# Chunk 0 of a delta-rule layer: the diagonal score blocks by products of their own, turned by VectorE, and loads in another order

## The chip, the cores and the metric

The kernel runs on one core of one Trainium2 chip. The metric is the device time of one execution in microseconds (us). Before the change it is 650.69 us, the median of three runs (650.61, 650.69 and 657.98).

## The reference

A linear attention with the delta rule (4 batches, 8 heads, 768 tokens, 48 elements a head) feeds a feed-forward block (3072 tokens, 384 wide, 2048 hidden):

```python
k_n = k / (np.linalg.norm(k, axis=-1, keepdims=True) + 1e-06)
state = np.zeros((B, H, D, D), dtype=np.float32)
for t in range(S):
    kt, vt, bt = (k_n[:, :, t], v[:, :, t], beta[:, :, t, None])
    y[:, :, t] = np.einsum('bhd,bhde->bhe', q[:, :, t], state)
    v_old = np.einsum('bhde,bhd->bhe', state, kt)
    state = state + bt[:, :, :, None] * np.einsum('bhd,bhe->bhde', kt, vt - v_old)
...
h = x @ w_in            # x: y with the heads side by side
g = h * (1.0 / (1.0 + np.exp(-h)))
return (g @ w_out).astype(np.float32)
```

## The kernel before

The tokens are cut into six chunks of 128. Within a chunk the recurrence is solved in closed form: each half of 64 tokens needs the inverse of a triangular 64x64 matrix made of the keys' products, beta and the keys' lengths. The inverse is built from 32x32 diagonal blocks: for each of the 32 pairs of batch and head and each of the four 32-token blocks, one 32x32 block stands on one partition of VectorE's layout (128 partitions of 1024 elements), and VectorE eliminates column after column there. Small matmuls of 32x32 tiles (`corner`, `turned`, `straight`, `merge_half`) then join the blocks. All matmuls are float32; one matmul of the program shows in the trace as two loads of weights and two matmuls.

What chunk 0 needs before its first state update is the start of the kernel:

- `load_k(0)` and `load_q(0)` bring keys and queries on SyncE's queue; beta comes on ScalarE's queue. `turn` (L481) transposes the keys of one batch b on TensorE, and VectorE or ScalarE copies them out of PSUM.
- `first_score` multiplies the keys of each 64-token half with themselves (`score`, L504) and copies the products into the tiles `ap`. `block_out` (L557) writes the 32x32 diagonal blocks of `ap` to DRAM in eight DMAs, and `block_in` reads them back, one block a partition, as `g`.
- `square` (L361) squares the keys on GpSimd, `add_squares` (L375) sums them on VectorE, and `norm_steps` (L383) makes from the sums the lengths `n` and the steps -beta/n^2 with some sixteen small VectorE instructions. `block_steps` (L430) brings the steps into the layout of the blocks with one TensorE product.
- `invert_first` (L651) multiplies the corners of `g` by the steps (L656), eliminates 15 columns (L664, L668), and transposes the result on VectorE (L678, L682). Between its steps TensorE turns the keys of chunk 1, and `busy` issues matmuls whose result nobody reads.
- `first_queries` turns the queries, multiplies keys by queries, and masks the result, on VectorE for the first half of the batches.
- `joins(0, ...)` runs the small matmuls of one half, with a list of things to do between its stages (parts of the narrowing of `w_in`, the scaling of v by `size_half`). Then follow `inner`, `first_outputs`, `update`, and the first hidden products (`phid`, L1029).

The order on each engine is the program's: `pin` ties each instruction to the one before it on its engine. DMAs of SyncE are in line as well; `linked` makes the next one wait until the last one before it has landed. The weights come as 768 KB pieces: `fetch_w_in(i)` loads, and `narrow` converts on ScalarE, VectorE and GpSimd.

PSUM has eight banks in three rotating groups, A (three), CC (three) and M (two); `bank(room, name)` takes the next of a group. The banks of CC are kept tiles, one each.

The order of loads behind the queries is

```python
    fetch_w_in(0)
    load_k(1)
    fetch_w_in(1)
    load_v(0)
    ...
    linked(fetch_w_in, 2)
    linked(load_q, 1)
    fetch_w_in(3)
    linked(fetch_w_in, 4)
```

and it stands behind `block_in(0)` in SyncE's queue.

Of the kernel before, what the change touches and what calls it, by code (L numbers as in the profile page):

```python
# [19 lines left out]
def kernel(  # L20
# [10 lines left out]
    nc = tc.nc  # L31
# [26 lines left out]
    A, CC, M = deque(("a0", "a1", "a2")), deque(("c0", "c1", "c2")), deque(("m0", "m1"))  # L58
    kept_banks = {tag: banks.tile([P, 512], FP32, name=f"pb_{tag}", tag=tag) for tag in CC}

    def bank(room, name):

        tag = room[0]
        room.rotate(-1)
        return kept_banks.get(tag) or banks.tile([P, 512], FP32, name=name, tag=tag)

# [101 lines left out]

    def linked(fetch, *args):

        pace.append(line[-1])
        fetch(*args)
# [173 lines left out]

    def beta_of(c):
        pb = bank(A, "pb")
        pin(nc.tensor.transpose(
            pb[:, 0:BH], beta_fm[:, c].rearrange("n s t -> n (s t)"), ident[0:BH, 0:BH]  # L350
        ))
        pin(nc.scalar.activation(
            out=beta_tok[:, c, :].rearrange("p (n e) -> p e n", e=2),
            in_=pb[:, 0:BH].rearrange("p (e n) -> p e n", e=2), func=ACTF.Copy,
        ))
# [26 lines left out]

    def norm_steps(c):  # L383

        seed, t, r = (small.tile([P, BH], kind, name=name, bufs=1)[:] for name, kind in (
            ("seed", U32), ("nt", FP32), ("nr", FP32)
        ))
        ss = sums.pop(c)
        n = small.tile([P, BH], FP32, name="n", bufs=1)
        by_slot = small.tile([P, 2, B * NP], FP32, name="n_slot", bufs=1)  # L390
        yield pin(nc.vector.tensor_scalar(
            out=seed, in0=ss.bitcast(U32), scalar1=-0.5, scalar2=1597463007.0,
# [12 lines left out]
        yield pin(nc.vector.tensor_tensor(out=t, in0=r, in1=ss, op=ALU.mult))  # L405
        yield pin(nc.vector.tensor_scalar(out=n[:], in0=t, scalar1=1e-6, scalar2=None, op0=ALU.add))
        yield pin(nc.vector.reciprocal(out=r, in_=n[:]))
        yield pin(nc.vector.tensor_tensor(out=t, in0=r, in1=beta_tok[:, c, :], op=ALU.mult))
# [133 lines left out]
    def block_room(c):  # L542

        if c == 0:
            g, x = (sum_room[:, at : at + T * T] for at in (AT_G, AT_X))
        else:
            g = work.tile([P, T * T], FP32, name="g", tag="g", bufs=1)[:]
            x = (
                sum_room[:, AT_LAST : AT_LAST + T * T] if c == 1
                else work.tile([P, T * T], FP32, name="x", tag="x", bufs=1)[:]  # L550
            )
        pin(nc.gpsimd.memset(x, 0.0))
        pin(nc.gpsimd.memset(x[:, 0 : T * T : T + 1], 1.0))
        g, x = (t.rearrange("p (s t) -> p s t", t=T) for t in (g, x))
        blocks[c] = (tc.dram_tile([P, T, T], FP32, name=f"blocks{c}"), g, x)

# [87 lines left out]

    Q, ys = T // 2, {}

# [4 lines left out]
    def invert_first(step):  # L651
# [33 lines left out]
        both = work.tile([P, BH, T], FP32, name="xe_y", tag="g", bufs=1)  # L685
        xes[0], ys[0] = both[:], both[:].rearrange("p (g h) t -> p g h t", g=2)

        def heads(g, hf):
            for i in range(HH // 2):
                for e in range(2):  # L690
                    yield i, HH * g + 2 * i + e, hf ^ e ^ g

        def of_half(t, g, hf, k):
            return t[:, HH * g + (hf ^ k ^ g) : HH * (g + 1) : 2]

# [3 lines left out]
        def corner(g, hf):  # L699

            pls = [bank(room, "pl") for room in (A, CC)]
            for i, n, k in heads(g, hf):
                for j in (2 * k, 2 * k + 1):
                    cols = slice(T * (j % 2), T * (j % 2 + 1))
                    pin(nc.tensor.matmul(
                        pls[k][rows[j], Q * i : Q * (i + 1)], lhsT=aps[0, g][0][rows[j], n % HH // H, n % H, cols],
                        rhs=low[rows[j], n, :], start=True, stop=True,
                    ))
                    yield
# [7 lines left out]
        def turned(g, hf):  # L717

            pls = [bank(room, "pl") for room in (A, CC)]
            for i, n, k in heads(g, hf):  # L720
                pin(nc.tensor.matmul(
                    pls[k][rows[2 * k], T * i : T * (i + 1)], lhsT=up[rows[2 * k], n, :],
                    rhs=y[rows[2 * k], n, :], start=True, stop=True,
                ))
                yield
# [3 lines left out]
        def straight(g, hf):  # L729

            pls = [bank(room, "pl") for room in (A, CC)]
            for i, n, k in heads(g, hf):
                for j in (2 * k + 1, 2 * k):
                    pin(nc.tensor.matmul(
                        pls[k][rows[j], T * i : T * (i + 1)], lhsT=y[rows[j], n, :],
                        rhs=up[rows[j], n, :], start=True, stop=True,
                    ))
                    yield
            for odd in (1, 0):
                for k, by in enumerate((by_act, by_dve)):  # L740
                    j = 2 * k + odd
                    by(
                        of_half(xi[rows[j]].rearrange("p g h t -> p (g h) t"), g, hf, k)[:, :, T * odd : T * odd + T],
                        out_of(pls[k], rows[j], T),
# [36 lines left out]
    def merge_half(g, hf, second):  # L781

        y = ys[0][:, g]
        pms = [bank(room, "px" if second else "py") for room in (A, CC)]
        for i in range(HH // 2):
            for e in range(2):
                n, k = 2 * i + e, hf ^ e ^ g
                even, odd = slice(W * k, W * k + T), slice(W * k + T, W * (k + 1))
                if second:
                    to, left, right = even, y[odd, n, :], xis[g][odd, n, T:W]  # L790
                else:
                    left = aps[0, g][0][even, n // H, n % H, T:W]
                    to, right = odd, xes[0][even, g * HH + n, :]
                yield pin(nc.tensor.matmul(
                    pms[k][to, T * i : T * (i + 1)], lhsT=left, rhs=right, start=True, stop=True
                ))
        for k, by in enumerate((by_act, by_dve)):
            e, half = hf ^ k ^ g, slice(W * k, W * k + T) if second else slice(W * k + T, W * (k + 1))
            of = pms[k][half, 0 : HH // 2 * T].rearrange("p (h t) -> p h t", t=T)
            by(xis[g][half, e::2, T:W] if second else y[half, e::2, :], of)  # L800

# [250 lines left out]
    def project():  # L1052

        rooms = [A.popleft(), CC.popleft()]
        pos = [bank(M, "po") for n in range(HB)]
        pos += [kept_banks.get(tag) or banks.tile([P, 512], FP32, name="po", tag=tag) for tag in rooms]
        o = mlp.tile([P, HB, DM], FP32, name="o", bufs=1)
# [204 lines left out]

    def first_score(b):

        def evacuate(j, e, to, of):
            (by_dve if e else by_act)(to, of)

        score(0, b, (0,), (A, CC), evacuate)
        if b % HB == 1:
            block_out(0, b // HB)  # L1270

    busy(3)
    for b in range(B):
        square(0, b)
    block_room(0)
    for b in range(2):
        turn(0, b, 0, M, b % 2 == 0)
    first_score(0)
    for b in range(2, B):
        turn(0, b, 0, M, b % 2 == 0)  # L1280
    for b in range(1, B):
        first_score(b)
        add_squares(0, b - 1)
    add_squares(0, B - 1)
    beta_of(0)

    def first_queries(b):

        def evacuate(j, e, to, of):
            (mask if b < HB else by_act)(to, of)  # L1290

        turn(0, b, 1, M)
        score(0, b, (1,), (A, CC), evacuate)

    block_in(0)
    busy(4)
    for _ in norm_steps(0):
        pass
    for b in range(2):
        first_queries(b)  # L1300
        busy(1)
    for t in xis:
        pin(nc.gpsimd.memset(t, 0.0))
    step = block_steps(0)
    fetch_w_in(0)
    load_k(1)
    fetch_w_in(1)
    load_v(0)
    for c in range(1, NCH):
        beta_of(c)  # L1310
    busy(1)
    for b in range(2, B):
        first_queries(b)
# [127 lines left out]
    sums_made = sum_w()  # L1441
    later = {}

    def script(text):
# [114 lines left out]
```

## Time and profile before

| what | value |
|---|---|
| runs | 650.61, 650.69, 657.98 us |
| profiled execution | 652.37 us, span 650.4 us |
| TensorE (PE) busy | 627.6 us, 96% of the span |
| VectorE (DVE) busy | 397.6 us, 61% |
| ScalarE (ACT) busy | 213.8 us, 33% |
| GpSimd (POOL) busy | 90.9 us, 14% |
| granted TensorE clock, mean | 0.99 |
| chain that ended last | PE 91%, DMA 2%, issue 2%, DVE 2% |
| inversion of chunk 0 (L656 to L682) | 20.71 to 34.03 us |
| first hidden product (L1029) | 52.3 us |

The times in the profile's rows are microseconds from the start of the span. A row of the chain gives start, duration and what it was; a row of the timeline gives start, busy time, engine, line, operation, output and inputs, and in brackets the idle time before it with what ended it. A row of the windows gives, after the stretch and its length, the busy time and number of instructions of PE, PE's weight loads, DVE, ACT and POOL, then the granted clock of TensorE, the DMA share, and GB/s. "Issue" is time in which the engine waited for nothing that the profile shows. PE's share is high, but the kernel's start is made of short dependent steps.

### The profile page before, as it was taken

What the parts mean: (1) busy time and instruction counts of PE and PEld (TensorE: products, weight loads), DVE (VectorE), ACT (ScalarE), POOL (GpSimd) and SP (SyncE); (2) the same over time, 40 slices, a digit from 0 to 9 for tenths busy, and PEclk for the clock granted to TensorE, in tenths of its full rate; (3) what the DMA queues carried; (4) which work ended last, traced back from release to release, by engine and by line L of the source; (5) the groups of instructions that cost most, each with busy time, mean ns of one, the idle gap of its engine ahead of it and who ended that gap; (6) DMA issues with size and microseconds to landing.
All of it is one profiled execution on the core that took longest, in us unless ns stands there. A gap on an engine that the chain in (4) does not pass through costs nothing.

```text
span 650.4 us, 21395 instructions
## 1 busy us (share of the span) xinstructions
PE 627.6 (96%) x9416; PEld 548.0 (84%) x9416; DVE 397.6 (61%) x911; ACT 213.8 (33%) x497; POOL 90.9 (14%) x92
## 2 busy tenths in 40 slices
PE   7878899999989999999999999999999999999997
PEld 5577778756779989989989989989989989889997
DVE  5875689997764987453986453987454974103112
ACT  2455663332342122451122452122451122451111
POOL 5023631334101020010020010020011000000000
PEclk9979999999989999999999999999999999999999
DMA  9876534250288324268324268324173024100101
GB/s 136 209 165 206 192 75 104 98 97 3 53 154 148 58 73 60 50 136 143 59 76 57 48 131 146 61 74 60 28 153 72 10 65 60 40 13 1 25 0 25
DMA packets 145676, 54.70 MB, mean 84 GB/s; under 512 B 117152, under 2 KB 138912, under 8 KB 145584
## 3 DMA queue, kind: packets, MB, share of 16 engines
q1 hardware_dynamic: 143136, 52.93, 39.6%
q8 instruction: 74, 1.21, 0.8%
q10 hardware_dynamic: 2448, 0.41, 0.4%
q14 instruction: 18, 0.15, 0.1%
HBM read 40.14 MB, written 11.01 MB: 79 GB/s over the span
## 4 chain that ended last, share of the span: by engine, by line
PE 91%; DMA 2%; issue 2%; DVE 2%; ACT 1%; SPq 1%; DVEq 0%
PE phid L1029 38%; PE px L1136 16%; PE py L1136 12%; PE po L1064 5%; PE pb_c L828 3%; PE pa L517 2%; PE pb_c L816 2%; PE pyc L907 2%; PE pb_c L1064 2%; PE pb_c L848 1%; PE pb_c L336 1%; PE pyc L894 1%; DMA kb<-in_k_dram 1%; PE pt L488 1%; PE py L770 1%
## 5 line engine op out<-in xcount | busy, mean ns | idle before, releaser
L1029 PE MATMUL phid<-xT,w_in 128*128 128x256 f32 x1152 | 260.1, 383 | 2.1 <-DMA xT<-part 2.0
L1029 PEld LDWEIGHTS phid<-xT,w_in 128*128 128x128 f32 x1152 | 216.9, 191 | 34.4 <-issue 3.0
L1039 ACT ACTIVATE gT<-phid 128x512 f32<-128x512 f32 x88 | 52.5, 597 | 149.8 <-PE phid L1029 145.2
L615 DVE SCALAR_TENSOR_TENSOR rank<-g,step,x 128x31 f32<-128x31 f32 (+15 forms) x124 | 49.8, 401 | 35.8 <-DMA g<-blocks 32.3
L1118 DVE TENSOR_TENSOR sums_of_g<-gT 128x384 f32<-128x384 f32 (+1 forms) x60 | 29.9, 518 | 59.0 <-ACT gT L1039 48.4
L1136 PE MATMUL py<-w_out,sums_of_g 128*128 128x192 f32 x320 | 56.8, 329 | 0.0
L1136 PE MATMUL px<-sums_of_w,sums_of_g 128*128 128x192 f32 x320 | 56.8, 329 | 0.0
L1136 PEld LDWEIGHTS px<-sums_of_w,sums_of_g 128*128 128x128 f32 x320 | 52.2, 190 | 0.5
L1136 PEld LDWEIGHTS py<-w_out,sums_of_g 128*128 128x128 f32 x320 | 52.2, 190 | 0.4
L620 DVE TENSOR_TENSOR x<-x,rank 128x31 f32<-128x31 f32 (+15 forms) x124 | 42.5, 343 | 4.3
L455 POOL TENSOR_TENSOR vf<-vf,n_slot 128x768 f32<-128x768 f32 x10 | 15.0, 1516 | 169.3 <-DMA vf<-in_v_dram 125.3
L476 DVE STREAM_TRANSPOSE kq<-stage 128x512 f32<-128x512 f32 x28 | 28.5, 1114 | 12.0 <-DMA stage<-in_q_dram 10.4
L532 ACT COPY xT<-pyc 48x128 f32<-48x128 f32 (+2 forms) x126 | 32.6, 259 | 1.6
L1136 PE MATMUL px<-sums_of_w,gT 128*128 128x192 f32 x160 | 28.4, 329 | 0.0
L1136 PE MATMUL py<-w_out,gT 128*128 128x192 f32 x160 | 28.4, 329 | 0.0
L1136 PE MATMUL px<-w_out,gT 128*128 128x192 f32 x160 | 28.0, 327 | 0.0
L1136 PEld LDWEIGHTS px<-w_out,gT 128*128 128x128 f32 x160 | 26.4, 190 | 0.5
L538 POOL COPY g<-x 64x256 f32<-64x256 f32 x4 | 5.0, 1241 | 154.5 <-DVE x L623 154.5
L1136 PEld LDWEIGHTS py<-w_out,gT 128*128 128x128 f32 x160 | 26.1, 190 | 0.3
L1136 PEld LDWEIGHTS px<-sums_of_w,gT 128*128 128x128 f32 x160 | 26.1, 190 | 0.2
L828 PEld LDWEIGHTS pb_c<-vf,xi 64*64 64x64 f32 x736 | 23.5, 138 | 3.2 <-issue 2.9
L1147 DVE TENSOR_TENSOR o<-o,kept 128x192 f32<-128x192 f32 (+1 forms) x29 | 11.5, 422 | 24.0 <-ACT kept L1144 24.0
(221 smaller groups left out, 921.6 us busy)
## 6 DMA issues: line engine op xcount, KB each, us to landing
vf<-in_v_dram SPq DMA_DIRECT2D x48, 96.0 KB, 3.2
out_dram<-o SPq DMA_DIRECT2D x42, 96.0 KB, 2.2
w_out<-in_moe_w_in_dram SPq DMA_DIRECT2D x4, 768.0 KB, 4.4
sums_of_w<-in_moe_w_out_dram SPq DMA_DIRECT2D x4, 768.0 KB, 5.9
blocks<-ap SPq DMA_DIRECT2D x44, 64.0 KB, 1.9
g<-blocks SPq DMA_DIRECT2D x5, 512.0 KB, 3.5
kb<-in_k_dram SPq DMA_DIRECT2D x12, 192.0 KB, 5.1
kb<-in_k_dram SPq DMA_DIRECT2D x24, 96.0 KB, 4.6
```

The costliest lines, as they stand in the source:

```text
L455: pin(nc.gpsimd.tensor_tensor(out=vf, in0=vf, in1=of, op=ALU.mult))
L476: pin(nc.vector.transpose(out=kqs[c, b][:, :, j, :].rearrange("p a (i m) -> p a m i", i=T), in_=src.rearrange("p a (m d) -> p a m d", d=D) ...
L517: pin(nc.tensor.matmul(pa[e][half, p * n * W : (p + 1) * n * W], lhsT=kq[rows, p, 0, half], rhs=kq[rows, p, js[0] : js[-1] + 1, half], sta ...
L532: return pin(nc.scalar.copy(to, of))
L615: pin(nc.vector.scalar_tensor_tensor(out=tv, in0=g[:, 0:m, m : m + 1].to_broadcast([P, m, n]), scalar=step[:, m : m + 1], in1=x[:, m : m + ...
L620: yield pin(nc.vector.tensor_tensor(out=x[:, 0:m, m:T], in0=x[:, 0:m, m:T], in1=tv, op=ALU.add))
L828: yield pin(nc.tensor.matmul(pz[rows, n * D : (n + 1) * D], lhsT=xis[g][rows, u * H + 2 * p + e, :], rhs=vfs[c][rows, hf, g * HB + u, p, : ...
L1029: pin(nc.tensor.matmul(ph[:, j * GT : (j + 1) * GT], lhsT=w_in[:, a, (2 * f + j) * P : (2 * f + j + 1) * P], rhs=xTs[c, hf][:, a, :], star ...
L1039: pin(nc.scalar.activation(out=hidden_of(c, hf, f), in_=ph[:], func=ACTF.Silu, scale=-0.5 if in_blocks(c) else 0.5))
L1064: pin(nc.tensor.matmul(pos[i][:, 0:DM], lhsT=hidden_of(0, hf, f // 2)[:, at : at + C], rhs=w_outs[f // HFF][:, f % HFF, :], start=(f == 0) ...
L1118: pin(nc.vector.tensor_tensor(out=sums_of_g[:, k, fs], in0=of[0], in1=of[1], op=op))
L1136: pin(nc.tensor.matmul(to, lhsT=at, rhs=quarter(f, *b) if isinstance(b, tuple) else sums_of_w[b][:, f], start=start and f == 0, stop=f == ...
```

## The change

In chunk 0 the round trip through DRAM is gone. `own_products(b)` multiplies, for each head and each 32-token block, the block's keys with themselves, 32 products a batch, into one PSUM tile `double` that spans two banks (the former c0 and c1 of CC, which later stages use as its two halves). One VectorE transpose of 128x1024 elements then brings all the 32x32 blocks into the layout of `g`. The blocks' diagonals are the squared lengths: one strided copy takes them, so that the squares on GpSimd and their sums on VectorE are left out in chunk 0. Beta is transposed by TensorE and once more by VectorE into the same layout, and the step comes from two more VectorE instructions, with no TensorE product. The lengths are brought back to tokens by one VectorE transpose behind the first step of the inversion, and ScalarE copies them into slots.

The key scores of whole halves are still made, behind the own products, in the banks of A and M, and ScalarE alone copies them out. The masks of chunk 0's first half move into `joins(0, ...)`. The order of the batch-and-head index in the joins follows the new layout. `busy` always uses bank c2. The loads of `w_in` 0 and of chunk 1's keys stand right behind the queries, and the others have new links: `linked` gets an argument `back`, which names how far back in SyncE's line the awaited DMA stands.

```diff
+    double = banks.tile([P, 1024], FP32, name="pb_c01", tag="c01")
+    kept_banks = {
+        "c0": double[:, 0:512], "c1": double[:, 512:1024], "c2": banks.tile([P, 512], FP32, name="pb_c2", tag="c2")[:],
+    }
...
-    def linked(fetch, *args):
-        pace.append(line[-1])
+    def linked(fetch, *args, back=1):
+        pace.append(line[-back])
         fetch(*args)
...
-            pw = bank(CC, "pw")
+            pw = kept_banks["c2"]
...
+    def own_products(b):
+        kq = kqs[0, b]
+        for p in range(NP):
+            for j in range(NB):
+                for e in range(2):
+                    n, of, at = HH * e + NP * b + p, slice(W * e, W * e + D), slice(T * j, T * (j + 1))
+                    pin(nc.tensor.matmul(
+                        double[at, T * n : T * (n + 1)], lhsT=kq[of, p, 0, at], rhs=kq[of, p, 0, at],
+                        start=True, stop=True,
+                    ))
+
+    def first_steps(pb):
+        by_head = small.tile([P, 2, T], FP32, name="by_head", bufs=1)
+        n, beta_n = (by_head[:, i] for i in range(2))
+        pin(nc.vector.transpose(out=beta_n, in_=pb[:, 0:BH]))
+        g = sum_room[:, AT_G : AT_G + T * T]
+        pin(nc.vector.transpose(
+            out=g.rearrange("p (t s) -> p t s", s=T), in_=double[:].rearrange("p (n t) -> p t n", t=T)
+        ))
...
+        pin(nc.vector.tensor_copy(out=ss, in_=g[:, 0 : T * T : T + 1]))
+        for _ in length_steps(ss, seed, t, r, n):
+            pass
+        pin(nc.vector.tensor_tensor(out=t, in0=r, in1=beta_n, op=ALU.mult))
+        step = small.tile([P, T], FP32, name="step")
+        pin(nc.vector.scalar_tensor_tensor(
+            out=step[:], in0=r, scalar=-1.0, in1=t, op0=ALU.mult, op1=ALU.mult
+        ))
+        return step, n
+
+    def first_sizes(n):
...
+        pin(nc.vector.transpose(out=by_token[:], in_=n))
...
     busy(3)
-    for b in range(B):
-        square(0, b)
     block_room(0)
     for b in range(2):
         turn(0, b, 0, M, b % 2 == 0)
-    first_score(0)
+    pb = turn_beta(0)
+    for b in range(2):
+        own_products(b)
     for b in range(2, B):
         turn(0, b, 0, M, b % 2 == 0)
-    for b in range(1, B):
-        first_score(b)
-        add_squares(0, b - 1)
-    add_squares(0, B - 1)
-    beta_of(0)
...
-    block_in(0)
-    busy(4)
-    for _ in norm_steps(0):
-        pass
...
-    step = block_steps(0)
+    for b in range(2, B):
+        own_products(b)
+    step, norms = first_steps(pb)
     fetch_w_in(0)
     load_k(1)
-    fetch_w_in(1)
-    load_v(0)
+    linked(load_v, 0, back=1 + 2 * 3)
+    for b in range(B):
+        score(0, b, (0,), (A, M), evacuated)
+    busy(2)
+    for t in xis:
+        pin(nc.gpsimd.memset(t, 0.0))
+    linked(fetch_w_in, 1, back=8 + 1)
...
-    linked(fetch_w_in, 2)
-    linked(load_q, 1)
-    fetch_w_in(3)
-    linked(fetch_w_in, 4)
-    linked(fetch_w_in, 5)
-    linked(fetch_w_in, 6)
+    linked(fetch_w_in, 2, back=2)
+    linked(fetch_w_in, 3, back=2)
+    linked(fetch_w_in, 4, back=2)
+    linked(load_q, 1, back=2)
+    linked(fetch_w_in, 5, back=2 * 3 + 1)
+    linked(fetch_w_in, 6, back=2)
     begin(("in", 0))
     inv = invert_first(step)
     for n in range(1 + Q):
         done = next(inv)
+        if n == 0:
+            first_sizes(norms)
...
-    together(joins(0, [sized, none, none, filled(2), filled(1), none, none, filled(2), begin_next, none]))
+    together(joins(0, [sized, none, none, filled(2), filled(1), masked, none, filled(2), begin_next, none]))
```

More of the change, by code (lines that the diff above doesn't have):

```diff
@@ new lines, in first_sizes @@
+    def first_sizes(n):
+        by_token = small.tile([P, BH], FP32, name="n", bufs=1)
+        by_slot = small.tile([P, 2, B * NP], FP32, name="n_slot", bufs=1)
+        pin(nc.vector.transpose(out=by_token[:], in_=n))
+        of = by_token[:].rearrange("p (e n) -> p e n", e=2)
+        for g, rows in enumerate(HALVES):
+            ns, rest = slice(HB * NP * g, HB * NP * (g + 1)), HALVES[1 - g]
+            by_act(by_slot[rows, :, ns], of[rows, :, ns])
+            for hf in range(2):
+                by_act(by_slot[rest, hf, ns], of[rest, 1 - hf, ns])
+        sizes[0] = by_slot
@@ L405, in norm_steps @@
         yield pin(nc.vector.tensor_tensor(out=t, in0=r, in1=ss, op=ALU.mult))
-        yield pin(nc.vector.tensor_scalar(out=n[:], in0=t, scalar1=1e-6, scalar2=None, op0=ALU.add))
-        yield pin(nc.vector.reciprocal(out=r, in_=n[:]))
+        yield pin(nc.vector.tensor_scalar(out=n, in0=t, scalar1=1e-6, scalar2=None, op0=ALU.add))
+        yield pin(nc.vector.reciprocal(out=r, in_=n))
+    def norm_steps(c):
+        seed, t, r = (small.tile([P, BH], kind, name=name, bufs=1)[:] for name, kind in (
+            ("seed", U32), ("nt", FP32), ("nr", FP32)
+        ))
+        ss = sums.pop(c)
+        n = small.tile([P, BH], FP32, name="n", bufs=1)
+        by_slot = small.tile([P, 2, B * NP], FP32, name="n_slot", bufs=1)
+        yield from length_steps(ss, seed, t, r, n[:])
         yield pin(nc.vector.tensor_tensor(out=t, in0=r, in1=beta_tok[:, c, :], op=ALU.mult))
@@ L641, in invert @@
         read_up(c, up)
-    Q, ys = T // 2, {}
+    Q, ys, later = T // 2, {}, {}
     def corners(at):
@@ L719, in turned @@
             pls = [bank(room, "pl") for room in (A, CC)]
-            for i, n, k in heads(g, hf):
+            for i, _, m, k in heads(g, hf):
                 pin(nc.tensor.matmul(
-                    pls[k][rows[2 * k], T * i : T * (i + 1)], lhsT=up[rows[2 * k], n, :],
-                    rhs=y[rows[2 * k], n, :], start=True, stop=True,
+                    pls[k][rows[2 * k], T * i : T * (i + 1)], lhsT=up[rows[2 * k], m, :],
+                    rhs=y[rows[2 * k], m, :], start=True, stop=True,
                 ))
@@ L1358, in none, with masked @@
         pass
-    together(joins(0, [sized, none, none, filled(2), filled(1), none, none, filled(2), begin_next, none]))
+    def masked():
+        for u in range(HB):
+            masks(0, u)
+    together(joins(0, [sized, none, none, filled(2), filled(1), masked, none, filled(2), begin_next, none]))
     masks(1, 0)
@@ L1441 @@
     sums_made = sum_w()
-    later = {}
     def script(text):
```

83 lines of the change are left out of this document (40 added, 43 removed).

## The prediction

> **What bounds it now.** The page comes first: PE is busy for 627.6 of 650.4 us and holds 91% of the chain that ended last. The change touches only the preparation of chunk 0, so what counts is when PE gets its first dense work, and how that start is limited. I read the chain of waits from 0 to 48 us, then VectorE's timeline, the 1-us windows, and the trace's packets of the queue that carries PE's program. The chain first:
>
> ```profile
> 5.17 3.35 DMA kb<-in_k_dram
> 9.84 0.20 PE pa L517
> 12.56 0.93 DVE ss L377 x2
> 13.52 0.19 DVE seed L391
> 16.21 0.36 DVE nr L407
> 17.49 0.19 DVE spread L411
> 20.07 0.14 PE pg L433 x2
> 34.20 0.29 issue
> 36.88 1.38 issue
> 40.52 1.86 issue
> ```
>
> Keys land, PE turns and multiplies them, VectorE adds squares, makes the step sizes, PE turns those, and the inversion can begin. The two long "issue" rows are PE waiting for nothing that the profile shows. VectorE's timeline has the inversion's start (L656), its last transpose, and the work that follows:
>
> ```profile
> 20.71 0.69 DVE L656 TENSOR_TENSOR sums_of_w<-sums_of_w,step 128x512 f32<-128x512 f32 x1 [0.95 <-ACT beta_tok L352]
> 31.19 1.06 DVE L678 STREAM_TRANSPOSE sums_of_w<-sums_of_w 128x512 f32<-128x512 f32 x1
> 32.10 1.93 DVE L682 STREAM_TRANSPOSE sums_of_w<-sums_of_w 128x1024 f32<-128x1024 f32 x1
> 44.81 1.29 DVE L1326 TENSOR_TENSOR ap<-ap,above 128x512 f32<-128x512 f32 x2
> ```
>
> The windows show PE empty in both issue rows, and the clock (seventh entry) halved behind the first; the trace has it at 0.5 from 39.64 to 49.88 us, three stretches of 3.41:
>
> ```profile
> 37.00:38.00 1.00, 0.00 (x0) 0.00 (x0) 0.56 (x1) 0.00 (x0) 0.01 (x1) 1.00 0.66 117
> 38.00:39.00 1.00, 0.73 (x67) 0.74 (x68) 0.33 (x1) 0.39 (x2) 0.00 (x0) 1.00 0.88 326
> 40.00:41.00 1.00, 0.52 (x20) 0.42 (x16) 0.97 (x3) 0.41 (x2) 0.32 (x1) 0.50 0.00 0
> 41.00:42.00 1.00, 0.00 (x0) 0.00 (x0) 0.76 (x2) 0.00 (x0) 1.00 (x1) 0.50 0.38 79
> ```
>
> **PE waits for its own program.** Page part 3 has a queue q8, kind instruction, of 74 packets; in the trace each has 16,384 bytes. I numbered PE's instructions (loads, matmuls, semaphore waits) in order of time. The issue stalls stand before numbers 1217, 1473, 2241, 2497, 2753 and 4033, all 193 plus a multiple of 256, and each ends 1.2 to 1.5 us after a q8 packet (40.94 to 42.37 for instance). Passing 193+256k asks for the block that is needed 256 later. From passing to use it took 3.73 us (34.53 to 38.26), 4.11 (38.26 to 42.37), 4.25, 4.55, and 6.86 when 2.3 MB of weights were in flight (60.50 to 67.36). So 256 small instructions cannot pass faster than about 4 us.
>
> [...]
>
> **The change, start of the inversion.** Removed: squares on POOL (4 x 0.82), VectorE's four reductions (L377, 0.54 each), eight block DMAs and the one back, the spread copies, the step product pg on PE and its ACT copy, and before the inversion 16 PE instructions net of own products (3 busy matmuls of 4, one pg of 4). POOL and SP work was in the way only through the waits above. Added: 128 own products, each two loads and two matmuls by the form of L517, so 512 PE instructions, 128 per b.
> - b 0 and 1: the first products can start where L517 starts now, 7.66. Beta's last packet ended at 6.23, so its transpose before them is not late. A score's 64 instructions take 7.66 to 8.14, 7.5 ns each; L705's 112 of 32-wide tiles take 51.58 to 52.07, 4.4 ns. With 0.8 us per b (bounds 0.56 and 0.96), two end at 9.3.
> - Turns of b 2 and 3 (keys landed at 8.53): first product 1.03 later, as 8.74 to 9.77 now. So 10.3, and b 2 ends at 11.1.
> - b 3 begins at number 436, and 449 stands 13 into it. Number 193, in b 1, passes at about 8.7; now it passes at 10.35, its packet ends at 13.40, and with 1.4 more the block is there 4.45 later. The same turnaround gives 13.15, plus 0.7 for the rest: 13.85. By 3.73 it is 13.1, by 6.86 it is 16.3; with no stall 11.9.
> - VectorE turns both banks, 128x1024. Rows of that size from SBUF take 1.93 to 1.97; from PSUM none is shown. Bounds: two copies of 128x512 out of PSUM (L500, 0.69 each), 1.4, and two transposes L476 of 1.114, 2.2. I take 1.95, the same operation: 15.8.
> - The diagonal copy 0.2, the unchanged length steps L391 to L407 3.15 (13.52 to 16.67), the product with beta and the step 0.43 as L408 and one L411: the inversion starts at **19.6**, not 20.71: 1.1 earlier (range 18 to 22).
> - One 128x32 transpose now stands inside the inversion, 0.2 by the small rows of L408. Its by-product, ACT's six size copies, is hidden: ACT is idle for 1.5 us at 28.7 and POOL needs the sizes only at 35.5; uncovered they cost 6 x 0.2.
>
> [...]
>
> **Joins.** Added and removed instructions net to +496 PE instructions, 16 short of two blocks, so every later boundary falls 16 instructions further on. Now the corners (L705) begin at number 716, 11 past a boundary that was passed early; after, the boundary comes 5 into them. The next block is then asked for at the corners rather than some 1.5 us ahead, and the sequence 34.5, 38.3, 42.4 becomes about 35.5, 39.5, 43.6 on the same scale: **1.2 lost** (0 to 2.4). The two masks of chunk 0's first half (1.29 us as the L1326 row) move from before the inversion into the joins; VectorE is idle there for 1.1 and 1.0 while PE waits for its block, so I cost them at 0; without those stalls they cost up to 1.3.
>
> **Loads.** Now w_in 2 to 6 and q 1 are chained from 36 to 59 us. After, SP's queue loses five block DMAs, so w_in 0 and k 1 follow q 0 at 9.8; v waits for w_in 0 (about 17), w_in 1 stands behind v's eight issues (0.65 each), and w_in 2 to 6 follow by landings: all in flight by about 43. Keys of chunk 1 stop holding PE (its wait ends at 29.35 now). No engine waits for weights between 30 and 110 us now, so earlier weights alone gain nothing; but fetches that queue behind them do. Stalls of 0.7, 1.4 and 1.9 us at 55.2, 59.1 and 65.5 meet DMA shares near 1. With quieter engines there, I take **1.7** of these 4.0 back (0 to 3.8). The price is busier DMA in the joins, inside the 1.2's upper bound.
>
> Sum: -1.1 + 0.2 + 1.2 - 1.7 = **-1.4 us**. The profiled execution took 652.37 (span 650.4, the rest around it), so it would take 651.0; the median shown, 650.69, lies 1.7 below that execution, and becomes **649.3**.
>
> **Rivals.**
> - The block is there in time for b 3, and later stalls go too (0.2). For: b 3 follows turns and copies, which give time. Against: 449 is reached at 11.2 and no block came within 3.7. Start at 17.7, 2.8 gained with the transpose inside, joins even, 1.7 to 3.5 later: 646.2 to 644.4.
> - Slower (0.2): fetches in the joins. Weights and q 1 are in flight at 31 to 43; if a turnaround there exceeds about 4.9 us, three boundaries cost three times the excess. At 6, 3 x 1.9 = 5.7 replaces the 1.2: 653.8. For: the 6.86 came with such traffic. Against: 4.11 came at shares of 0.9.
> - The start comes earlier but the time doesn't (0.1): the fetch pace and not VectorE sets 34 to 67 us, and the quieter DMA gives nothing: 650.7.
> - The half clock lasts one stretch longer or shorter (part of the range): 3.41 at half rate is at most 1.7 either way.
>
> The forecast itself has 0.5. Two per cent, 13 us, is about what a measurement of this kernel can tell from no change; every case lies within it, so 0.95 falls there, 0.02 faster and 0.03 slower for what I have not seen, such as a wait on the two banks made into one tile. The range is 645 to 653: most of the first rival, and of the slower one the part with a turnaround up to about 5.7.
>
> **What would show it.** Right: 512 PE instructions at 7.7 to 14 us with an issue gap of 1 to 2 us before the last b; one 128x1024 VectorE transpose of about 1.95 at 14; L656's successor at 19 to 20; issue rows in the joins no shorter than now; fewer after 55. Wrong: an inversion start before 18.5 or after 21, a transpose far from 1.95, joins over 12 us after the corners, or ACT late with key copies so that the corners wait for scores.

## The result, and the profile after

The change makes the kernel slower: 688.25 us, the median of four runs (683.37 to 689.83), against 653.42 for the kernel before in runs made beside them. The ratio is 1.0513, with a 95% interval from 1.0422 to 1.0605. The forecast was 649.3 us within 645 to 653. The profiled execution of the changed kernel took 689.83 us, with a span of 688.1. Ratios here and below are of undisturbed runs only, so they are not always the quotient of the two medians.

The chain of waits of the changed kernel, in the stretch that the prediction showed of before (start, duration, what):

```profile
10.90 0.79 PE pb_c L399 x47
11.69 2.35 issue
14.04 0.79 PE pb_c L399 x44
14.83 2.28 PE pa L577 x69
17.11 2.58 issue
19.69 1.97 PE pa L577 x59
21.65 2.86 PE pb_c L339 x4
...
36.08 3.42 PE pb_c L339 x10
...
43.19 0.13 PE pl L771 x2
...
45.36 1.75 issue
```

The own products (L399) meet the block boundary of the program as forecast (2.35 us). But the chain then stays with TensorE (PE), and ScalarE's copies of the queries between its products, for 28 us. The key scores (L577) stand behind the own products and meet the next boundary (2.58). Then come two warming products that take 2.86 us, the queries one batch after the other, and the warming products of chunk 1, until the first corner (L771) at 43.12 (its piece of the chain begins at 43.19). VectorE's timeline of the same kernel shows who waits meanwhile:

```profile
14.87 1.25 DVE L410 STREAM_TRANSPOSE sums_of_w<-pb_c 128x1024 f32<-128x1024 f32 x1 [3.90 <-PE pb_c L399]
19.91 0.69 DVE L717 TENSOR_TENSOR sums_of_w<-sums_of_w,step 128x512 f32<-128x512 f32 x1
31.32 1.89 DVE L743 STREAM_TRANSPOSE sums_of_w<-sums_of_w 128x1024 f32<-128x1024 f32 x1
43.87 0.34 DVE L778 SCALAR_TENSOR_TENSOR sums_of_w<-pl,second,pick 64x128 f32<-64x128 f32 x1 [10.66 <-PE pb_c L771]
52.92 2.57 DVE L1374 TENSOR_TENSOR ap<-ap,above 128x512 f32<-128x512 f32 x2
```

The inversion starts at 19.91 (before: 20.71) and ends at 33.21 (before: 34.03). So the round trip through DRAM is indeed replaced by something quicker. Then VectorE is idle for 10.66 us, because the corners are not there; in before it went on at once. The waits over the whole span (engine, tile and line, what it waited for; us in total, times, longest), first the four longest of PE on VectorE in after, then the longest of these in the kernel b_double, which matters below:

```profile
PE pb_c L577 <- DVE ap L587: 6.9, 4, 2.8
PE pb_c L860 <- DVE xi L595: 4.7, 3, 2.5
PE pb_c L800 <- DVE xe_y L595: 1.6, 2, 1.1
PE pb_c L771 <- DVE sums_of_w L778: 0.8, 1, 0.8
```

```profile
PE pb_c L520 <- DVE ap L530: 3.7, 4, 1.4
```

`pb_c` is a bank of the group CC, of which c0 and c1 are now halves of one tile. The products wait until VectorE has copied something out of it, at places far from chunk 0 too: 2.8 us of the first row stand at about 215 us, 2.1 at about 512. The page's row of the granted clock, first of after, then of a_apart (below), shows what follows from such gaps:

```profile
PEclk9796689999999999999999999999999999989999
```

```profile
PEclk8796999999999999999999999999999999999999
```

In the trace the clock of after is at 0.5 for 58.0 us in all, in seven stretches that are multiples of 3.41 us (the first from 14.14 to 24.38, the next from 48.28 to 65.34); before has 13.7 us. The products of `phid` (L1095) start every 0.43 us from 215.6 to 218.8, at 0.50, and every 0.22 us from 224 to 226, at 1.00. So by an estimate from the granted clock the 44 us more cost at most half of that, 22 us of the 37.7 by which the spans differ.

Where the time goes, by the start of each stage (us in the span of the profiled execution; the kernels are explained below):

| kernel | inversion | first corner | first `inner` | first `phid` | span | ratio to before (95%) |
|---|---|---|---|---|---|---|
| before | 20.71 | 33.37 | 44.24 | 52.34 | 650.4 | 1 |
| after | 19.91 | 43.12 | 59.06 | 67.34 | 688.1 | 1.0513 (1.0422 to 1.0605) |
| b_double | 21.38 | 35.11 | 49.92 | 57.91 | 672.4 | 1.0287 (1.0246 to 1.0329) |
| a_apart | 19.05 | 42.02 | 55.76 | 63.56 | 659.6 | 1.0139 (1.0098 to 1.018) |
| a_pipe | 19.91 | 36.99 | 52.57 | 60.45 | 680.2 | 1.037 (1.0319 to 1.0421) |
| a_loads | 20.02 | 43.34 | 56.46 | 64.44 | 679.6 | 1.0466 (1.0409 to 1.0522) |
| both | 19.67 | 36.35 | 50.86 | 58.34 | 652.7 | 1.0006 (0.9972 to 1.004) |
| both_pad | 18.95 | 37.33 | 51.42 | 59.80 | 655.1 | 1.0045 (1.0006 to 1.0084) |
| both_warm | 18.87 | 34.28 | 48.58 | 56.29 | 653.4 | 0.9995 (0.9966 to 1.0025) |
| both_masks | 19.44 | 34.46 | 46.68 | 56.20 | 654.5 | 1.0041 (1.0002 to 1.008) |
| both_quiet | 20.02 | 35.44 | 45.65 | 61.95 | 657.9 | 1.0146 (1.0089 to 1.0203) |
| both_loads | 19.76 | 37.12 | 50.69 | 58.45 | 655.8 | 1.0049 (1.0022 to 1.0077) |
| both_q1 | 19.65 | 34.79 | 46.00 | 55.39 | 649.7 | 0.9987 (0.9947 to 1.0027) |
| both_q1_nopad | 19.00 | 33.64 | 45.11 | 54.18 | 653.7 | 1.0048 (1.0013 to 1.0084) |

The first `phid` of after comes 15.0 us late, yet the end comes 37.7 us late. So 22.7 us are lost behind the stage that the change touches.

### The profile page after: what moved, and what is told of

It reads as the page before. It is cut to its first block, busy times and chain, and to the rows that moved or that the text cites. A ratio compares the mean times of both kernels' runs of the same rounds, so it can differ in the third digit from the quotient of the medians.

```text
span 688.1 us, 21853 instructions
## 1 busy us (share of the span) xinstructions
PE 647.3 (94%) x9664; PEld 563.3 (82%) x9664; DVE 393.8 (57%) x896; ACT 216.9 (32%) x509; POOL 87.6 (13%) x88
## 3 DMA queue, kind: packets, MB, share of 16 engines
q8 instruction: 76, 1.25, 0.8%
## 4 chain that ended last, share of the span: by engine, by line
PE 87%; DVE 5%; issue 3%; ACT 2%; SPq 1%; DMA 1%; POOL 1%; DVEq 0%; POOLq 0%; ACTq 0%
PE phid L1095 37%; PE px L1202 15%; PE py L1202 11%; PE po L1130 3%; PE pb_c L894 3%; PE pa L577 2%; PE pb_c L339 2%; PE pb_c L882 2%; PE pb_c L914 1%; PE pb_c L577 1%; PE pt L548 1%; PE pyc L973 1%; SPq L161 1%; PE pyc L960 1%; DMA stage<-in_q_dram 1%
## 5 line engine op out<-in xcount | busy, mean ns | idle before, releaser
L1095 PE MATMUL phid<-xT,w_in 128*128 128x256 f32 x1152 | 267.7, 392 | 1.8 <-DMA xT<-part 1.7
L1095 PEld LDWEIGHTS phid<-xT,w_in 128*128 128x128 f32 x1152 | 223.0, 196 | 35.3 <-issue 4.3
L1105 ACT ACTIVATE gT<-phid 128x512 f32<-128x512 f32 x88 | 52.5, 597 | 159.1 <-PE phid L1095 152.5
L515 POOL TENSOR_TENSOR vf<-vf,n_slot 128x768 f32<-128x768 f32 x10 | 14.8, 1484 | 172.5 <-DMA vf<-in_v_dram 125.4
L894 PEld LDWEIGHTS pb_c<-vf,xi 64*64 64x64 f32 x736 | 25.1, 145 | 6.8 <-issue 3.3
L894 PE MATMUL pb_c<-vf,xi 64*64 64x48 f32 x736 | 27.3, 230 | 2.9 <-ACT z L592 2.3
L577 PE MATMUL pa<-kq 48*64 48x128 f32 (+1 forms) x448 | 24.3, 279 | 5.3 <-ACT kq L558 2.7
L577 PEld LDWEIGHTS pa<-kq 48*64 48x64 f32 x448 | 20.6, 158 | 8.0 <-issue 4.1
```

Source lines behind the costliest of these rows:

```text
L515: pin(nc.gpsimd.tensor_tensor(out=vf, in0=vf, in1=of, op=ALU.mult))
L577: pin(nc.tensor.matmul(pa[e][half, p * n * W : (p + 1) * n * W], lhsT=kq[rows, p, 0, half], rhs=kq[rows, p, js[0] : js[-1] + 1, half], sta ...
L894: yield pin(nc.tensor.matmul(pz[rows, n * D : (n + 1) * D], lhsT=xis[g][rows, u * H + 2 * p + e, :], rhs=vfs[c][rows, hf, g * HB + u, p, : ...
L1095: pin(nc.tensor.matmul(ph[:, j * GT : (j + 1) * GT], lhsT=w_in[:, a, (2 * f + j) * P : (2 * f + j + 1) * P], rhs=xTs[c, hf][:, a, :], star ...
L1105: pin(nc.scalar.activation(out=hidden_of(c, hf, f), in_=ph[:], func=ACTF.Silu, scale=-0.5 if in_blocks(c) else 0.5))
```

## Experiments, first round: which part of the change costs

Three theories stood against each other: T1, the two halves of one tile make products wait for copies that have nothing to do with them; T2, TensorE's queue ahead of the corners has become longer than the inversion; T3, the arrival of the program's blocks and the half clock.

**a_apart**: after, with c0 and c1 as tiles of their own from the moment that VectorE has turned the double tile. The instructions stay; the two warming products behind the key scores write to c0 and c1.

```diff
-    double = banks.tile([P, 1024], FP32, name="pb_c01", tag="c01")
+    first = ExitStack()
+    double = first.enter_context(tc.tile_pool(name="first", bufs=1, space=PSUM)).tile([P, 1024], FP32, ...)
...
     step, norms = first_steps(pb)
+    first.close()
+    pair = ctx.enter_context(tc.tile_pool(name="pair", bufs=1, space=PSUM))
+    for tag in ("c0", "c1"):
+        kept_banks[tag] = pair.tile([P, 512], FP32, name=f"pb_{tag}", tag=tag)
...
-    busy(2)
+    busy(2, tags=("c0", "c1"))
```

> The changed kernel, but the two banks of the own products are one tile only until VectorE has turned them; from then on c0 and c1 are two tiles again, and the two busy matmuls behind the key scores go to c0 and c1. Theory T1 (the shared tile: a wait on either half is a wait on both, in the joins and in every later chunk's scores): the joins, 16.0 us from the first corner to the last merge in the changed kernel, fall to 12 or less, the waits of TensorE on VectorE's masked scores (3.1 us in the window around 215 us, 2.4 around 512) are gone, and the time falls by 15 us or more, to 664 to 673. Theory T2 (TensorE's queue ahead of the corners alone) and T3 (program fetch and clock): within 4 us of 688; the first corner stays at 43 us under all three.

Measured: 662.9 us, ratio 1.0139. The first corner stays at 42.02, as T1 has it, and about 25 us are gone, a little more than T1's bound. No score waits for VectorE in this kernel, and from 60.6 us on the clock stays at 1.0 to the end, with 23.9 us of half clock in all. The joins, from first corner to first `inner`, fall from 15.9 to 13.7 us, not to the 12 that T1 expected. The pages show what the 28.5 us between the two spans are made of: the same 9664 matmuls keep TensorE busy for 647.3 us in after and for 630.9 in a_apart, 16.4 us less, and the time in which it is not busy falls by 12.1 us.

**b_double**: before, with nothing but the two banks made into halves of one tile.

```diff
+    double = banks.tile([P, 1024], FP32, name="pb_c01", tag="c01")
-    kept_banks = {tag: banks.tile([P, 512], FP32, name=f"pb_{tag}", tag=tag) for tag in CC}
+    kept_banks = {"c0": double[:, 0:512], "c1": double[:, 512:1024], "c2": banks.tile([P, 512], ...)[:]}
```

> The kernel before with one edit: banks c0 and c1 are the two halves of one tile, as in the change; nothing else. T1: slower by 8 us or more, in the joins (10.9 us now from the first corner to the last merge) and at the scores of later chunks. T2 and T3: the time of the kernel before within 2 us, since neither TensorE's queue nor its number of instructions is touched.

Measured: 673.89 us beside 654.95 for before, ratio 1.0287: 19 us for a change that adds no instruction. Four waits of scores on VectorE appear here too (3.7 us, the row above), and the joins take 14.8 us instead of 10.9. T1 holds from both sides: put in alone it costs 19 us, taken out of after it gives 25 back.

**a_pipe**: after, with the queries' serial chain (turn, ScalarE's copy, score, then the next batch) overlapped by two batches, and the four warming products between them left out.

```diff
     for b in range(2):
         turn(0, b, 1, M)
-        score(0, b, (1,), (A, CC), evacuated)
-        busy(1)
     for c in range(1, NCH):
         beta_of(c)
-    for b in range(2, B):
-        turn(0, b, 1, M)
+    for b in range(B):
         score(0, b, (1,), (A, CC), evacuated)
-        busy(1)
+        if b + 2 < B:
+            turn(0, b + 2, 1, M)
```

> The changed kernel with chunk 0's queries in another order: two batches are turned ahead, each further turn stands behind a score, and the four busy matmuls between them are left out (their result is read by nobody). T2 (turn, copy, score and busy of four batches run one after the other for 11.6 us, from 24.5 to 36.1, and push the corners to 43.1 while VectorE waits for 10.7): the four batches take 6 to 7 us, the first corner comes at 37 to 39, and the time falls by 4 to 7 us. T3 (fetch): the fetch pace holds the corners, which move by less than 2 us. T1 says nothing of the corners.

Measured: 679.51 us, ratio 1.037; the first corner at 36.99 instead of 43.12. The gain against after is 8.7 us, a little over what T2 gave.

**a_loads**: after, with the loads in before's order and with its links.

> The changed kernel with the loads in the order and with the links of the kernel before (they still stand ahead of the key scores, with no round trip of blocks before them). If the new order of loads delays the program's blocks (packets 2.4 and 1.8 us behind the passing at 14.0 and 19.7 us), the two stalls of 2.5 and 2.6 us shorten and the time falls by 2 to 5 us; if the order helps, as the prediction had it, the time grows by 1 to 4 us; T1 and T2 alone leave it within 2 us.

Measured: 685.57 us, ratio 1.0466. The interval overlaps that of after, so this run alone settles nothing; both_loads takes it up again. The two stalls ahead of the inversion did not shorten: from one TensorE instruction's start to the next they are 2.6 and 3.2 us, in after 2.5 and 2.9.

## Experiments, second round: do the two causes account for the whole loss?

Four kernels, each with one edit more than the one before it.

**both**: the edits of a_apart and a_pipe together.

> After with two edits: the two halves become tiles of their own once VectorE has turned them (as in a_apart), and the queries' turns and scores overlap by two b, four warming products left out (as in a_pipe). Theory T1 (shared tile) and T2 (TensorE's queue ahead of the corners) add up: a_apart is at 662.9 with the first corner at 42.0; the corner should come at about 36 as in a_pipe (36.99), and 5 to 6 us of that should reach the end: 657 to 659. Rival: the end of the joins is set by something that does not move with the corners (the program's blocks, loads, the masks), then the joins get longer by what the corners gain, as in a_pipe (15.6 us from first corner to the first product of the inner stage, against 13.7 in a_apart), and the time is 660 to 663.

Measured: 653.4 us beside 653.85, ratio 1.0006 with an interval from 0.9972 to 1.004. This is better than the expectation. The two edits together take back all of the loss that was measured, and the change as a whole then neither gains nor loses anything measurable. That is a sum of two parts: by the table the first `phid` of both still comes 6.0 us later than in before, and the rest of the span takes 594.3 us instead of 598.1 (one profiled execution each; the runs spread by some microseconds).

**both_pad**: both, with `pad(20)` behind the queries' scores: 20 tiny products whose result nobody reads.

> The kernel both with 20 tiny products (32x32 by 32x16, into a bank that nobody reads) ahead of the corners, about 40 instructions of TensorE. They change only where the program's 256-instruction boundaries fall: the first corner moves from 19 instructions before the boundary 1217 to about 20 behind it, so that the next block has been fetched while TensorE waits. Theory T3 (the program's blocks): in after, a_apart and a_pipe the joins run over 1473, 1729 and 1985 and stall at each (2.5, 1.6 and 1.3 us in a_apart), before over 1217 and 1473 alone; with the boundaries moved the stall at 1473 should go and the joins be 1.3 to 2.5 us shorter, the time 1 to 2.5 us under both. Rival: the stalls are the loads' traffic or the two arrays' waits, then the joins keep their length within 0.5 us and the time stays within 1 us.

Measured: 657.53 us, ratio 1.0045: the time does not fall but is likely some 3 us more than that of both, which neither case of the expectation had (the intervals overlap). The joins keep their length within 0.5 us (14.1 us for 14.5). T3 in this form fell. Each tiny product takes four of TensorE's instructions, so that the corners now start at number 1275 instead of 1196, 58 behind a boundary. The boundaries inside the joins are two instead of three, but the two stalls are 1.7 and 4.75 us, 6.4 in all; in both the three were 2.2, 3.25 and 1.4, 6.9 in all. What counted here was how long a block takes, not how many boundaries there are.

**both_warm**: both_pad, with warming products where TensorE waits for its program, and 15 tiny products instead of 20.

```diff
+    busy(3)
     for b in range(2, B):
         own_products(b)
...
+    busy(2)
+    busy(2, tags=("c0", "c1"))
     for b in range(B):
         score(0, b, (0,), (A, M), evacuated)
-    busy(2, tags=("c0", "c1"))
```

> The kernel both_pad (15 tiny products instead of 20) with warming products where TensorE waits for its program: three ahead of the own products of b = 2, and two, with the two that fill the halves, ahead of the key scores instead of behind them. Theory: the half clock from 12.9 to 23.1 us in a_apart comes from TensorE's idle time at the two block waits (1.8 and 2.5 us), and it doubles the key scores, the warming products and the turns; kept busy, TensorE stays at 1.0, the two products behind the key scores (2.7 us at half clock) are gone from the path, and the first corner comes 2 to 4 us earlier, at 32.5 to 34.5 (not before the inversion's end, 32.3). Time 2 to 3 us under both_pad. Rival: the queries' copies by ScalarE set the corners, whatever the clock: the corner moves by under 1 us, and so does the time.

Measured: 654.05 us, ratio 0.9995. The half clock of 13.4 to 23.6 us is gone (1.0 from 5.5 to 39.6), and the first corner comes at 34.28, 3.05 earlier. The time falls by 3.5 us by the medians, a little more than expected. VectorE's row of the first corner, in both and then in both_warm, gives its remaining wait:

```profile
37.19 0.34 DVE L779 SCALAR_TENSOR_TENSOR sums_of_w<-pl,second,pick 64x128 f32<-64x128 f32 x1 [4.13 <-PE pb_c L772]
```

```profile
35.03 0.34 DVE L786 SCALAR_TENSOR_TENSOR sums_of_w<-pl,second,pick 64x128 f32<-64x128 f32 x1 [2.81 <-PE pb_c L779]
```

**both_masks**: both_warm, with the two masks put ahead of the joins. The expectation speaks of 2.4 to 2.6 and 1.29 us each; these are the busy times of both masks together.

> The kernel both_warm with the two masks of VectorE (128x512 each) taken out of the joins and put ahead of them, where VectorE waits for the corners. Theory: in the joins they take 2.4 to 2.6 us each beside GpSimd's addition of 1.84 us and stand in front of the evacuations of the merges; ahead of the corners they take 1.29 each and are hidden by the wait for the corners, and the joins are 1 to 2.5 us shorter: time 1 to 2.5 us under both_warm. Rival: in the joins VectorE waits for TensorE anyway (the block stalls), then the joins keep their length within 0.5 us; and if the corners now come as early as the inversion's end, the masks stand in front of the corners' evacuations and cost up to 2.6 us.

Measured: 654.82 us, ratio 1.0041. The joins (first corner to first `inner`) shrink from 14.3 to 12.2 us as expected, but the first `phid` stays at 56.20 and the time does not fall: from the first `inner` to it both_masks takes 9.5 us and both_warm 7.7. What sets this end was not settled. The masks and what GpSimd does beside them, first in both_warm, where they stand in the joins:

```profile
43.63 2.56 DVE L1387 TENSOR_TENSOR ap<-ap,above 128x512 f32<-128x512 f32 x2
```

```profile
43.22 1.82 POOL L241 TENSOR_TENSOR w_in<-w_in,raw 128x768 int32<-128x768 int32 x1 [5.84 <-DMA sums_of_g<-in_q_dram]
```

and in both_masks, ahead of them:

```profile
32.68 1.25 DVE L1387 TENSOR_TENSOR ap<-ap,above 128x512 f32<-128x512 f32 x2
```

```profile
32.92 1.42 POOL L1400 MEMSET sums_of_w<- 128x1584 f32 x1 [3.56 <-DVE sums_of_w L751]
```

Beside an addition of two tiles on GpSimd the two masks together take twice their time; beside a memset they don't.

## Experiments, third round: the program's blocks, the loads, and a better kernel

**both_quiet**: both_masks, with the loads of `w_in` 3 to 6 and of chunk 1's queries held until the joins are done.

```diff
-    linked(fetch_w_in, 3, back=2)
-    ...
-    linked(fetch_w_in, 6, back=2)
...
     together(joins(0, [sized, none, none, ...]))
+    pace.append(pins[seen_on])
+    fetch_w_in(3)
+    linked(fetch_w_in, 4, back=2)
+    ...
```

> The kernel both_masks with the loads of w_in from number 3 on and of chunk 1's queries held back until VectorE has finished the first half's joins, so that from about 36 to 47 us no load runs beside TensorE's program. Theory T3, as the last four kernels leave it: a 256-instruction block is asked for when the block before is entered, and takes 1.1 us until its packet starts where the loads are quiet (a_apart at 47.1 and 50.6), but 2.6 to 4.2 us beside the loads (both at 42.9, both_pad at 46.4); without the loads the stalls in the joins shrink from 1.6 and 3.4 us to about 1 each, the joins last 10 to 10.5 us instead of 12.2, and the first product of the inner stage starts at 44.5 to 45. The end then depends on whether w_in is missed 10 us later: 651 to 654 if not, up to 664 if the in-projection waits. Rival: the packets come late for another reason (each block's turnaround is what it is): the joins stay at 12 us or more.

Measured: 660.42 us, ratio 1.0146, within the expectation's upper case. The windows (length; busy time of PE, its weight loads, VectorE, ScalarE, GpSimd; clock, DMA share, GB/s) of both_masks and then of both_quiet:

```profile
34.00:46.00 12.00, 7.25 (x433) 6.50 (x433) 6.74 (x15) 5.13 (x13) 3.63 (x3) 0.78 0.87 208
```

```profile
34.00:46.00 12.00, 9.30 (x463) 8.29 (x463) 8.23 (x18) 6.74 (x15) 4.20 (x3) 0.75 0.02 5
```

With the DMA engines at 2% instead of 87%, a block's packet starts 0.8 to 1.1 us after TensorE has entered the block before it; in both_masks it was 1.2 to 2.9. The stalls in the joins are 0.8 and 2.15 us instead of 1.6 and 3.4, and the joins last 10.2 us instead of 12.2. So the loads do delay TensorE's program. The price stands in the chain of both_quiet:

```profile
46.21 4.79 DMA w_out<-in_moe_w_in_dram
...
52.66 4.74 DMA sums_of_g<-in_q_dram
```

The queries of chunk 1 land at 57.4. TensorE's turns wait 6.9 us for them, and the first `phid`, which stands behind these turns, starts at 61.95.

**both_loads**: both, with the loads in before's order.

> The kernel both with the loads in the order and with the links that they have in before (as a_loads, but with the shared tile and the queue mended). a_loads was 2.7 us under after, with overlapping intervals. If the order itself costs, this is 1 to 4 us under both; if the order that the change brings is worth something, 1 to 4 us over it; if it was noise of that run, within 1.5 us (my expectation, 0.6).

Measured: 656.09 us, ratio 1.0049 (1.0022 to 1.0077) against 1.0006 (0.9972 to 1.004) for both. The order that the change brings is worth about 2.7 us by the medians. The intervals overlap a little, so the sign is likely and the size is not settled; my own expectation, noise, was the less likely one.

**both_q1**: both_quiet, with chunk 1's queries loaded ahead of the held loads.

> The kernel both_quiet with chunk 1's queries loaded ahead of the held loads, behind w_in number 2: in both_quiet they landed at 57.4 and TensorE's next turns waited for them (first product of the MoE at 61.95 instead of 56.2). Theory: that wait was the whole price of holding the loads; the queries now land by 42, the joins stay at 10 to 11.5 us because most of their time is still quiet, and the first product of the MoE comes at 53.5 to 55: time 2 to 3 us under both_masks, 651.5 to 653. Rival: the parts of w_in that come 10 us later are missed next, or the stages behind give the gain back: 654 to 657.

Measured: 653.94 us beside 654.31, ratio 0.9987. The joins last 11.2 us, but the first `phid` comes at 55.39, not 53.5 to 55: behind the joins the held loads now stand beside TensorE's program, which stalls for 1.35 us at 52.5. The time is at the lower end of the rival's range.

**both_q1_nopad**: both_q1 without `pad(15)`.

> The kernel both_q1 without the 15 tiny products, so that the first corner stands again near the boundary 1217 (by about 60 instructions less). If what counts in the joins is the boundaries' number, they last 1 to 2 us longer than in both_q1 and the time is 1 to 2 us more; if with quiet loads TensorE's program comes at its own pace of about 3.4 us for a block whatever the phase, the joins change by less than 0.7 us and the time by less than 1.

Measured: 654.92 us, ratio 1.0048. The joins last 11.5 us instead of 11.2, within 0.7, as the theory of the block's own pace has it. The time is 1.0 us more by the medians and 0.6% by the ratios, with intervals that overlap, so it decides nothing. The first `phid` comes 1.2 us earlier, and a half-clock stretch of 3.41 us at 569 us, which both_q1 doesn't have, takes up to 1.7. No version beats before by more than the interval.

## Why the prediction was wrong

**The unpriced wait on the two banks** is the largest error. The prediction names it among the things not seen, with 0.03, and gives it no time. The runs give it 19 us (b_double) to 25 us (after against a_apart). It is not the waits alone: those of the four rows shown add up to 14 us, and the clock halves beside such gaps (58.0 us of it in after, 23.9 in a_apart). Of the 28.5 us of span that a_apart gives back, 16.4 are matmuls that run faster and 12.1 are waits that are gone. It could have been bounded beforehand. The corners, joins and scores all take the next bank of CC in turn, and the copies out of a bank are single rows of 0.34 to 0.43 us, in chunk 0 and in all chunks behind it. The statement that the change touches only the preparation of chunk 0 was wrong: its tile lives to the end of the kernel.

**The corners' other side** was not followed. The sum counts what the change adds to TensorE ahead of the inversion, but not what was already queued there. The prediction reads the chain of before as running through the inversion. Between its rows at 20.07 and 34.20 that chain has products of TensorE and copies of ScalarE, and no step of the inversion:

```profile
26.32 3.42 PE pb_c L336 x10
29.75 0.44 PE pt L488 x4
...
33.00 0.44 PE pt L488 x4
33.44 0.14 PE pl L705 x2
...
34.12 0.08 DVE sums_of_w L712
```

In before the queries' chain began at about 13.9 us and met the inversion with nothing to spare: VectorE's last transpose ended at 34.03 and the copy of the first corner began at 34.12. So an inversion that ends earlier could not by itself bring the corners forward. Own products up to 14.83, key scores up to 21.65 and two warming products up to 24.5 push the same chain behind the inversion's end, and the first corner comes 9.9 us after that end. The chain's first instruction starts at 23.66 instead of 13.86, 9.80 us later, and from there to the first corner it takes 19.5 us in both kernels. The queue was moved as a whole. The prediction named a sign close to this, ScalarE late with key copies so that the corners wait for scores. What came was the corners waiting, but for their place in TensorE's queue and not for key copies, and the sum has no price for it. Mended, it gives 8.7 us (a_pipe).

**Start of the inversion**: right, 19.91 for 19.6, but in part by luck, since two terms were off against each other. The first own product starts at 8.24, not 7.66, since VectorE's copy of the keys ends only then, and the block at number 449 is there at 14.04, not 13.15, so the own products end at 14.83 for 13.85. The transpose of both banks takes 1.25 us, not 1.95, and less than the lower bound of 1.4. The rows of 1.93 to 1.97 that I took have their input in SBUF, and this one reads PSUM. From its end to the inversion 3.79 us pass, forecast 3.78.

**Joins**: 15.9 us from first corner to first `inner` in after instead of 10.9, over the 12 that the prediction names as a sign of being wrong; forecast +1.2. Of the 5.0, 2.2 belong to the shared tile (13.7 in a_apart); put into before alone it costs 3.9 there (b_double). The masks, costed at 0, are busy for 2.57 us in the joins (the row at 52.92 above) and are worth about 2.1 (both_warm against both_masks). The loads beside the program's blocks are about 2.0 (both_masks against both_quiet). The last two are differences between mended kernels, so they need not add up exactly. The count of boundaries on which the 1.2 rested did not matter (both_pad).

**Loads**: the 1.7 us was right in kind, as far as it can be told: both_loads is 2.7 us over both. The stalls at block boundaries from 55 to 75 us, which the prediction put at 4.0 in before, are 0.4 us in both and 1.9 in both_loads, which fits the mechanism that it names. In after the gain is buried under the rest.

**Rivals**: none of them was the case. The slower one had its mechanism partly right (blocks delayed by loads in the joins, some 2 us), and by its sum it would have ended at 653.8.

## What to carry to other kernels

Joining two rotating banks into one tile for the sake of one instruction put the waits of both on later uses here, far behind the stage that needed it (19 us in b_double). Give the banks back as tiles of their own as soon as that instruction is done, and price the joined tile by every place that rotates through it, to the end of the kernel. Where work is put ahead in an engine's fixed order, look for the next meeting point of two chains and ask by how much the other chain was ahead there: here by nothing, so that 0.8 us won by the inversion came with 9.8 us lost by the corners.

## What the runs showed of the hardware

Short waits can cost more than their length. In after, stretches of half clock that are multiples of 3.41 us start in gaps between TensorE's matmuls or behind them, 58.0 us in all against 13.7 in before. A gap of 2.84 us that ends at 214.36 is followed by one stretch from 215.53; not every gap is, for none follows the 1.20 us at 113.94. Warming products in two gaps removed 10.2 us of half clock (both_warm).

Two VectorE multiplications of SBUF tiles (the masks, 128x512 each) take 2.56 us together while GpSimd adds two SBUF tiles (both_warm), and 1.25 us while GpSimd only fills one (both_masks). In both_warm GpSimd's addition starts 0.41 us earlier and ends at 45.04. The first mask takes 1.96 us and ends at 45.59, 0.55 us after the addition; the second takes 0.68. In after it is the same: the addition ends at 54.34, the first mask takes 1.97 us and ends at 54.89, the second takes 0.68. Whether the first mask waits for the addition or runs slower beside it was not shown.

TensorE's program comes late beside loads: from the entry into one block to the packet of the next it took 0.8 to 1.1 us with the DMA engines at 2% (both_quiet), and up to 4.2 us beside loads (both_pad). In before it took 4.40 us (60.50 to 64.90) at a DMA share of 1.03.
